# Retention chunks in plain float32 on half arrays, with the decay factored out of the mask

## The chip, the cores and the metric

One core of a Trainium2 chip. The time is the device time of one execution in microseconds; the times before are those of three runs, and one further execution was profiled.

## The reference

Three stages in a row, all in float32. The diff touches the first alone.

```python
# 1. retention; batch 2, 8 heads, 768 steps, head size 64
gamma = 1.0 - 2.0 ** (-5.0 - np.arange(H))
for t in range(S):
    state = gamma[None, :, None, None] * state + einsum('bhd,bhe->bhde', k[:, :, t], v[:, :, t])
    y[:, :, t] = scale * einsum('bhd,bhde->bhe', q[:, :, t], state)
# 2. mixture of experts, one expert of 8 for each of the 1536 tokens, with a capacity of 384
expert_idx = np.argmax(x @ w_gate, axis=1)      # tokens go to their expert's slots in order
y = np.maximum(disp[e] @ w1[e], 0) @ w2[e]      # 512 -> 1024 -> 512, for each expert
out[i] = gate_w[i] * y[expert_idx[i], pos[i]]
# 3. four experts, all of them for every token
out += p[:, e:e + 1] * (np.maximum(x @ w1[e], 0.0) @ w2[e])
```

## The kernel before, in words

The order of the instructions on each engine is that of the program text; each engine takes its instructions in that order, and nothing reorders them but the waits for data and buffers.

Retention works on 12 chunks of 128 steps (6 for each batch; `NCH` = 6, `NT` = 12). For a chunk `i`, all eight heads at once, there are these steps, named by their functions:

- `st_Q`: splits the transposed q and k, each 128 x 512, into a high and a low part of the type fp32r, so that products of nearly float32 precision come from three fast passes. The q parts are put into `qpad`, which is zero wherever a head's other partner has its rows, so that a pair of heads shares one 128-row product. ScalarE writes the high part of q (line 215), VectorE subtracts for the low part (line 216, two instructions of 64 x 512 for each chunk); k's parts are by ScalarE (line 207) and GpSimd (line 208).
- `st_S`: the products of q and k (line 258, twelve instructions, columns 256 wide), into two banks of PSUM, and from there into `sd` with a product with `dec` (VectorE, line 264), which is the causal mask and the decay inside the chunk together, a table of 128 x 1024. GpSimd makes `kg`, which is k times a power of the decay (line 238), and `qg`, which is q times one (line 246).
- `st_U`: k times v summed over the chunks of a batch, in one bank that is held (line 280), copied by ScalarE to the state `st` (line 288). The last chunk of a batch (c = 5) needs none.
- `st_O`: the state product, called I in what follows (line 298, not for the first chunk of a batch), and sd times v (line 308), called O, into one bank, copied to `xT` by ScalarE (line 317).
- `x_pe`: called X; xT is transposed, with the logits beside it, by four products with `iw` (line 339). VectorE reduces the logits (line 345, 353), ScalarE copies the rows to `xk` (line 349), SP writes them to `xd` in memory (line 352).
- `x_dve`, `r_pe`, `r_dve`, `g_pe`: choice of the expert, rank of the token in it, slot lists: many small operations, nearly all on VectorE.

One trip `it` of the loop takes U and O of chunk `it - 1`, S of chunk `it`, the splits of chunk `it + 1`, the loads of chunk `it + 3`, X of chunk `it - 2`, the slots of chunk `it - 4` and the ranks of chunk `it - 3`, in this order. In trips 8 and 9 a block of weights of the second stage is split besides (ScalarE line 106, VectorE line 107). Loads of q and k, and of k and v, go through pools of three buffers each, all on SP's queue. After the loop come O(11), with X(10) and the ranks of 9 between its two halves, then the slots, a gather of the first expert's rows from `xd` (`gidx0`, line 468; `xe0`, line 471), and the first expert's transposed input, whose parts come from the gather (line 498) and from the last two chunks in place (line 489).

The rest of the kernel is the two stages of experts, three fp32r passes each, products of 224 columns for the slots of an expert in the second stage (lines 804 and 828) and of 512 in the third (lines 857 and 878).

Of the kernel before, what the change touches and what calls it, by code (L numbers as in the profile page):

```python
# [37 lines left out]
C_GK = C_D + 1024  # L38
# [12 lines left out]
def tile_retention_moe_moe(ctx: ExitStack, tc, qkv, cst, gqt, a1, a2, b1, b2, dp, out, cap):  # L51
# [89 lines left out]
    with ExitStack() as actx:  # L141
        pa = actx.enter_context(tc.tile_pool(name="pa", bufs=1))
        pq = actx.enter_context(tc.tile_pool(name="pq", bufs=3))
# [4 lines left out]
        gqs = pa.tile([P, NCH - 1, 512], F32, name="gqs")  # L148
# [3 lines left out]
        dec = cdec[:, C_D:C_GK].rearrange("p (j x) -> p j x", j=2)  # L152
# [6 lines left out]

        qpad = [pa.tile([P, 2, 4, 2, P], F32R, name=f"qpad{b}") for b in range(2)]  # L160
# [16 lines left out]
        nc.vector.memset(qpad[0].bitcast(F32), 0.0)  # L177
        nc.gpsimd.memset(qpad[1].bitcast(F32), 0.0)
        load_qk(0)
        load_kv(0)  # L180
        nc.sync.dma_start(out=cdec, in_=cst[:, 0:C_IW])
        load_qk(1)
        load_kv(1)
        load_gq(0)
        load_qk(2)
        nc.sync.dma_start(out=iw.rearrange("p a b -> p (a b)"), in_=cst[:, C_IW:C_U])
        load_kv(2)
        load_gq(1)
# [11 lines left out]
        def st_Q(i):  # L200
            qk = qk_t[i]
            qT = qk[:, 0].rearrange("p (h t) -> p h t", h=4)
            ks = p2.tile([P, 2, 512], F32R, tag="ks", name=f"ks{i}")
            live[i] = {"ks": ks}
            qp = qpad[i % 2]
            def split_k():
                (nc.scalar.copy if i > 1 else nc.vector.tensor_copy)(ks[:, 0], qk[:, 1])
                nc.gpsimd.tensor_tensor(
                    out=ks[:, 1], in0=qk[:, 1], in1=ks[:, 0].bitcast(F32), op=ALU.subtract
                )  # L210

            def split_q():
                for j in range(2):
                    r = slice(64 * j, 64 * j + 64)
                    nc.scalar.copy(qp[r, 0, :, j], qT[r])  # L215
                    nc.vector.tensor_tensor(  # L216
                        out=qp[r, 1, :, j], in0=qT[r], in1=qp[r, 0, :, j].bitcast(F32),
                        op=ALU.subtract,
                    )

            if i == 2:
                split_q()
                split_k()
            else:
                split_k()
                split_q()

        def st_S(i):
            qk = qk_t.pop(i)
            kv = kv_t.pop(i)  # L230
            c = i % NCH
            d = live[i]
            d["v"] = kv[:, 1]
            ks = d.pop("ks").rearrange("p s (h t) -> p s h t", h=4)
            qp = qpad[i % 2].rearrange("p s h j t -> p s h (j t)")
            if c < NCH - 1:
                kg = p2.tile([P, 8, HD], F32, tag="kg", name=f"kg{i}")
                nc.gpsimd.tensor_tensor(
                    out=kg, in0=kv[:, 0].rearrange("p (h d) -> p h d", h=8),
                    in1=gk[:, c].rearrange("p (h d) -> p h d", d=1).to_broadcast([P, 8, HD]),  # L240
                    op=ALU.mult,
                )
                d["kg"] = kg
            if c > 0:
                qg = p2.tile([P, 512], F32, tag="qg", name=f"qg{i}")
                (nc.vector if i < 3 else nc.gpsimd).tensor_tensor(
                    out=qg, in0=qk[:, 0], in1=gqs[:, c - 1], op=ALU.mult
                )
                d["qg"] = qg
            sd = p2.tile([P, 2, 512], F32, tag="sd", name=f"sd{i}")  # L250
            d["sd"] = sd
            bks = [bank(f"S{i}_{g}") for g in range(2)]
            steps = [(n, hp) for hp in range(4) for n in range(3)]
            if i < 3:
                steps.sort()
            for n, hp in steps:
                a, b = PASS[n]
                nc.tensor.matmul(  # L258
                    out=bks[hp // 2][:, (hp % 2) * SL:(hp % 2 + 1) * SL],
                    lhsT=ks[:, a, hp], rhs=qp[:, b, hp], start=(n == 0 and hp % 2 == 0),  # L260
                    stop=True, skip_group_check=True,
                )
            for g in range(2):
                nc.vector.tensor_tensor(out=sd[:, g], in0=bks[g], in1=dec[:, g], op=ALU.mult)
# [3 lines left out]
        def st_U(i):  # L268
            c = i % NCH
            if c == NCH - 1:  # L270
                return
            if c == 0:
                u_ps[0] = bank(f"U{i}", "u")
            u = u_ps[0][:, 0:KD * HD].rearrange("p (a d) -> p a d", a=KD)
            kg = live[i].pop("kg")
            v = live[i]["v"]
# [12 lines left out]

        def st_O(i, between=None):  # L290
            d = live[i]
            c = i % NCH
            bk = bank(f"O{i}")
            sd, v = d.pop("sd"), d.pop("v")
            if c > 0:
                qg = d.pop("qg")
                for hp in range(4):
                    nc.tensor.matmul(
                        out=bk[:, hp * P:(hp + 1) * P], lhsT=st[c % 2][:, hp],
                        rhs=qg[:, hp * P:(hp + 1) * P], start=(hp == 0), stop=False,  # L300
                        skip_group_check=True,
                    )
            if between:
                between()
            for hp in range(4):
                for j in range(2):
                    h = 2 * hp + j
# [22 lines left out]
        def x_pe(i):  # L330
# [21 lines left out]
            nc.sync.dma_start(out=xd[1 + i * P:1 + (i + 1) * P], in_=xk)  # L352
# [70 lines left out]
        for it in range(NT):  # L423
            if it >= 1:
                st_U(it - 1)
                st_O(it - 1)
            if it == 0:
                st_Q(0)
            st_S(it)
            if it + 1 < NT:  # L430
                st_Q(it + 1)
            if it + 3 < NT:
                load_qk(it + 3)
                if it + 2 < NCH - 1:
                    load_gq(it + 2)
                load_kv(it + 3)
# [23 lines left out]
        def between():  # L460
            x_pe(NT - 2)
            r_pe(NT - 3)

        st_O(NT - 1, between)
# [440 lines left out]
def consts(cap):  # L905
# [8 lines left out]
    dm = np.zeros((P, 4, 2, P))  # L914
# [3 lines left out]
    for hd in range(H):  # L918
        hp, j = divmod(hd, 2)
        g = g32[hd]  # L920
        dm[:, hp, j] = np.where(t >= s, scale * g ** np.maximum(t - s, 0), 0.0)
        gk[:, :, hd] = g ** -(ch[None, :] + s + 1.0)
        gq[:, j, :, hp] = scale * g ** (ch[:, None, None] + t[None] + 1.0)
    c[:, C_D:C_GK] = dm.reshape(P, 1024)
# [8 lines left out]
    return c, gq[1:].astype(np.float32).reshape(NCH - 1, P, 512)  # L933
# [61 lines left out]
```

## Time and profile before

| | |
|---|---|
| median of three runs | 802.54 us (801.21 to 802.81) |
| the profiled execution | 802.98 us |
| its span, first to last instruction | 801.2 us |
| mean granted TensorE clock | 0.993 |
| TensorE busy | 779.7 us, 97% of the span |
| VectorE, ScalarE, GpSimd busy | 338.7, 224.7, 93.4 us |

A busy time is the sum of the times from an instruction's start to its end; matmuls overlap in the array and their ends are modelled, so a group's start to the next group's start says what it costs TensorE. A float32 matmul is two records in this trace, an fp32r one is one. PE is TensorE, PEld its weight loads, DVE VectorE, ACT ScalarE, POOL GpSimd; SPq is SP's queue of transfers. The granted clock is a share of 2.4 GHz.

### The profile page before, as it was taken

To read this page: it belongs to the slowest core of one execution; us is meant where nothing else is said; L and a number is where in the kernel's file an instruction comes from. 1 tells how busy PE (TensorE), PEld (TensorE's weight loads), DVE (VectorE), ACT (ScalarE), POOL (GpSimd) and SP (SyncE) were. 2 spreads that over 40 slices of the span, in tenths; PEclk is the share of its full clock that TensorE was granted. 3 is DMA by queue.
4 is the path that set the end of the run, shared out by engine and by line. 5 is a ranking of instruction groups with operands and counts; after the bars stand their busy time and mean duration, and the time that the engine had idled before them with its cause. 6 is when DMAs were issued, how large, how long until landed. Compare 5 with 4: busy or idle time off the path is not lost.

```text
span 801.2 us, 11248 instructions
## 1 busy us (share of the span) xinstructions
PE 779.7 (97%) x4700; PEld 678.9 (85%) x4701; DVE 338.7 (42%) x550; ACT 224.7 (28%) x351; POOL 93.4 (12%) x81
## 2 busy tenths in 40 slices
PE   8987899999999999999999999999999999999996
PEld 5876899999999988888888888888888888888886
DVE  7999786766666531212351221243121235122121
ACT  5555455555545320202230110312020223011010
POOL 6564323212200000000000000000000000000101
PEclk9999999999999999999999999999999999999999
DMA  9784567676666510000150000033000011000001
GB/s 325 268 275 160 171 220 261 208 221 204 209 187 186 183 53 1 1 0 1 53 157 1 1 0 1 5 105 101 1 0 1 1 53 52 27 27 13 40 2 51
DMA packets 24873, 76.64 MB, mean 96 GB/s; under 512 B 4945, under 2 KB 5217, under 8 KB 24818
## 3 DMA queue, kind: packets, MB, share of 16 engines
q1 hardware_dynamic: 20016, 68.21, 26.2%
q0 software_dynamic: 2672, 7.44, 2.9%
q8 instruction: 38, 0.62, 0.3%
q10 hardware_dynamic: 2130, 0.23, 0.2%
q14 instruction: 17, 0.14, 0.1%
HBM read 69.53 MB, written 6.34 MB: 95 GB/s over the span
## 4 chain that ended last, share of the span: by engine, by line
PE 87%; issue 1%; DMA 0%; POOLq 0%; DVE 0%
PE n L857 33%; PE n L878 32%; PE m L804 11%; PE m L828 11%; PE T L678 1%; DMA out_dram<-acc,tl 0%; POOLq L991 0%; DVE acc L889 0%; POOLq L894 0%
## 5 line engine op out<-in xcount | busy, mean ns | idle before, releaser
L857 PE MATMUL n<-x2h,w 128*128 128x512 f32 x768 | 238.4, 389 | 0.0
L857 PEld LDWEIGHTS n<-x2h,w 128*128 128x128 f32 x768 | 144.2, 188 | 30.0
L857 PE MATMUL n<-x2l,w 128*128 128x512 f32 x384 | 149.4, 389 | 0.0
L107 DVE TENSOR_TENSOR w<-raw,w 128x1024 fp32r<-128x1024 f32 x96 | 118.6, 1245 | 18.6 <-ACT w L106 18.5
L106 ACT CAST w<-raw 128x1024 fp32r<-128x1024 f32 x96 | 98.3, 1046 | 0.5 <-DVE tmpc L728 0.4
L889 DVE SCALAR_TENSOR_TENSOR acc<-n,tl,acc 128x512 f32<-128x512 f32 (+1 forms) x37 | 27.3, 737 | 156.7 <-PE n L878 156.7
L804 PE MATMUL m<-xet,w 128*128 128x224 f32 x768 | 88.9, 277 | 2.1 <-issue 1.7
L804 PEld LDWEIGHTS m<-xet,w 128*128 128x128 f32 x768 | 88.1, 195 | 2.4 <-issue 1.8
L857 PEld LDWEIGHTS n<-x2l,w 128*128 128x128 f32 x384 | 72.1, 188 | 14.9
L894 POOL DMA_INDIRECT out_dram<-acc,tl x12 | 11.5, 962 | 571.0 <-DVE acc L889 571.0
L787 ACT ACTIVATE g_0h<-n 128x512 fp32r<-128x512 f32 x12 | 7.2, 598 | 252.7 <-PE n L857 252.7
L258 PE MATMUL S<-qpad,ks 128*128 128x256 f32 x144 | 23.8, 301 | 9.4 <-DVE qpad L216 8.8
L216 DVE TENSOR_TENSOR qpad<-qk,qpad 64x512 fp32r<-64x512 f32 x24 | 31.4, 1307 | 2.3 <-ACT qpad L215 1.9
L258 PEld LDWEIGHTS S<-qpad,ks 128*128 128x128 f32 x144 | 18.8, 191 | 14.5 <-DVE qpad L216 11.3
L884 DVE TENSOR_SCALAR acc<-n,tl 128x512 f32<-128x512 f32 x12 | 9.0, 751 | 51.2 <-PE n L878 51.2
L878 PE MATMUL n<-w,g_1h 128*128 128x512 f32 (+1 forms) x98 | 29.8, 385 | 0.0
L878 PE MATMUL n<-w,g_2h 128*128 128x512 f32 (+1 forms) x98 | 29.8, 385 | 0.0
L878 PE MATMUL n<-w,g_7h 128*128 128x512 f32 (+1 forms) x98 | 29.8, 385 | 0.0
L878 PE MATMUL n<-w,g_3h 128*128 128x512 f32 (+1 forms) x98 | 29.7, 385 | 0.0
L878 PE MATMUL n<-w,g_4h 128*128 128x512 f32 (+1 forms) x98 | 29.7, 385 | 0.0
L878 PE MATMUL n<-w,g_5h 128*128 128x512 f32 (+1 forms) x98 | 29.7, 385 | 0.0
L878 PE MATMUL n<-w,g_6h 128*128 128x512 f32 (+1 forms) x98 | 29.7, 385 | 0.0
(186 smaller groups left out, 1220.7 us busy)
## 6 DMA issues: line engine op xcount, KB each, us to landing
raw<-a SPq DMA_DIRECT2D x64, 512.0 KB, 4.2
raw<-b SPq DMA_DIRECT2D x32, 512.0 KB, 3.6
qk<-qkv SPq DMA_DIRECT2D x12, 512.0 KB, 5.8
kv<-qkv SPq DMA_DIRECT2D x12, 512.0 KB, 5.5
xd<-xk SPq DMA_DIRECT2D x12, 256.0 KB, 3.7
gqs<-gqt SPq DMA_DIRECT2D x5, 256.0 KB, 6.1
cdec<-cst SPq DMA_DIRECT2D x1, 536.0 KB, 5.9
iw<-cst SPq DMA_DIRECT2D x1, 272.0 KB, 7.4
```

Of the source, the lines that this page charges most:

```text
L106: nc.scalar.copy(w[:, 0], r)
L107: nc.vector.tensor_tensor(out=w[:, 1], in0=r, in1=w[:, 0].bitcast(F32), op=ALU.subtract)
L216: nc.vector.tensor_tensor(out=qp[r, 1, :, j], in0=qT[r], in1=qp[r, 0, :, j].bitcast(F32), op=ALU.subtract,)
L258: nc.tensor.matmul(out=bks[hp // 2][:, (hp % 2) * SL:(hp % 2 + 1) * SL], lhsT=ks[:, a, hp], rhs=qp[:, b, hp], start=(n == 0 and hp % 2 == ...
L678: nc.tensor.transpose(bks[g][:, (2 * q + b) * P:(2 * q + b + 1) * P], t[:, b, (2 * g + q) * P:(2 * g + q + 1) * P], ident,)
L804: nc.tensor.matmul(out=bk[:, ff * SL:ff * SL + SM], lhsT=w[:, sw, k, ff * P:(ff + 1) * P], rhs=x[:, sx, k, 0:SM], start=(k == 0 and n == 0 ...
L828: nc.tensor.matmul(out=bk[:, q * SL:q * SL + SM], lhsT=w[:, sw, k], rhs=hs[k // 2][sh][:, hcols], start=(k == 0 and n == 0), stop=(k == KF ...
L857: nc.tensor.matmul(out=bk, lhsT=w[:, sw, k, ff * P:(ff + 1) * P], rhs=x2[sx][:, k, g * 512:(g + 1) * 512], start=(k == 0 and n == 0), stop ...
L878: nc.tensor.matmul(out=bk[:, 0:width], lhsT=hs[k][sh][:, t * P:(t + 1) * P], rhs=w[:, sw, k % 2, cols], start=(k == 0 and n == 0), stop=(k ...
L884: nc.vector.tensor_scalar(out=acc[i][:, cols], in0=bk[:, 0:width], scalar1=sc, scalar2=None, op0=ALU.mult,)
L889: nc.vector.scalar_tensor_tensor(out=acc[i][:, cols], in0=bk[:, 0:width], scalar=sc, in1=acc[i][:, cols], op0=ALU.mult, op1=ALU.add,)
L894: nc.gpsimd.indirect_dma_start(out=out, out_offset=bass.IndirectOffsetOnAxis(ap=tl[:, i, 4:5].bitcast(I32), axis=0), in_=acc[i], in_offset ...
```

## The change

The decay g^(t-s) between two steps of a chunk is written as g^(t+1) times g^-(s+1), with the powers counted from the start of the batch. The second factor goes into v (`vg`, GpSimd, where `kg` was), the first one and the scale are applied to the finished output (`gqs`, now for all six chunks), and of `dec` there is left a causal mask of zeros and ones, 128 x 128, read for all heads. The constants that are loaded with it shrink from 536 KB to 88 KB and go to ScalarE's queue.

With no decay inside, q and k go into the products as they are loaded: `st_Q`, `qpad`, `ks` and `qg` are gone, and the products of q and k are float32 matmuls on 64 rows, the even heads of the pairs on rows 0 to 63 and the odd ones on rows 64 to 127, each into a bank of its own. U takes k and vg, O takes vg and sd, I takes q itself.

The state product has its own function `st_I`, ahead of U in a trip. The output of chunks 0 to 9 is copied by ScalarE from its bank to `ot`, and multiplied by `gqs` to `xT` on GpSimd; of chunks 10 and 11 VectorE multiplies straight from the bank (chunk 11 in two halves). The pools of the loads have five buffers each, and the write of `xk` to `xd` is issued by ScalarE in place of SP.

```diff
-        pq = actx.enter_context(tc.tile_pool(name="pq", bufs=3))
+        pq = actx.enter_context(tc.tile_pool(name="pq", bufs=5))
...
-        dec = cdec[:, C_D:C_GK].rearrange("p (j x) -> p j x", j=2)
+        causal = cdec[:, C_D:C_GK].rearrange("p (o t) -> p o t", o=1).to_broadcast([P, 4, P])
...
         load_qk(0)
+        nc.scalar.dma_start(out=cdec, in_=cst[:, 0:C_IW])
         load_kv(0)
-        nc.sync.dma_start(out=cdec, in_=cst[:, 0:C_IW])
         load_qk(1)
+        load_gq(0)
         load_kv(1)
...
-        def st_Q(i):
...
         def st_S(i):
             qk = qk_t.pop(i)
             kv = kv_t.pop(i)
             c = i % NCH
...
+            vg = p2.tile([P, 8, HD], F32, tag="vg", name=f"vg{i}")
+            nc.gpsimd.tensor_tensor(
+                out=vg, in0=kv[:, 1].rearrange("p (h d) -> p h d", h=8),
+                in1=gk[:, c].rearrange("p (h d) -> p h d", d=1).to_broadcast([P, 8, HD]),
+                op=ALU.mult,
+            )
             sd = p2.tile([P, 2, 512], F32, tag="sd", name=f"sd{i}")
...
+            live[i] = {"sd": sd, "vg": vg, "k": kv[:, 0], "q": qk[:, 0]}
+            bks = [bank(f"S{i}_{j}") for j in range(2)]
+            for hp in range(4):
+                cols = slice(hp * P, (hp + 1) * P)
+                for j in range(2):
+                    r = slice(64 * j, 64 * j + 64)
+                    nc.tensor.matmul(
+                        out=bks[j][:, cols], lhsT=qk[r, 1, cols], rhs=qk[r, 0, cols],
+                        start=True, stop=True,
+                    )
+            for j in range(2):
+                nc.vector.tensor_tensor(
+                    out=sd[:, j].rearrange("p (h t) -> p h t", h=4),
+                    in0=bks[j].rearrange("p (h t) -> p h t", h=4), in1=causal, op=ALU.mult,
+                )
...
-                        out=u[64 * j:64 * j + 64, hp], lhsT=kg[:, h],
-                        rhs=v[:, h * HD:(h + 1) * HD], start=(c == 0 and hp == 0),
+                        out=u[64 * j:64 * j + 64, hp], lhsT=k[:, h * HD:(h + 1) * HD],
+                        rhs=vg[:, h], start=(c == 0 and hp == 0),
...
+        def st_I(i):
             c = i % NCH
-            bk = bank(f"O{i}")
-            sd, v = d.pop("sd"), d.pop("v")
+            bk = live[i]["o"] = bank(f"O{i}")
+            q = live[i].pop("q")
             if c > 0:
...
+        def st_O(i):
...
                     nc.tensor.matmul(
                         out=bk[64 * j:64 * j + 64, hp * P:(hp + 1) * P],
-                        lhsT=v[:, h * HD:(h + 1) * HD],
-                        rhs=sd[:, h // 4, (h % 4) * P:(h % 4 + 1) * P],
+                        lhsT=vg[:, 2 * hp + j], rhs=sd[:, j, hp * P:(hp + 1) * P],
                         start=(c == 0 and hp == 0), stop=True, skip_group_check=True,
                     )
             xT = p2.tile([P, 512], F32, tag="xT", name=f"xT{i}")
-            w = 256 if i == NT - 1 else 512
-            for o in range(0, 512, w):
-                nc.scalar.copy(xT[:, o:o + w], bk[:, o:o + w])
+            if i < NT - 2:
+                ot = p2.tile([P, 512], F32, tag="ot", name=f"ot{i}")
+                nc.scalar.copy(ot, bk)
+                nc.gpsimd.tensor_tensor(out=xT, in0=ot, in1=gqs[:, c], op=ALU.mult)
+            else:
+                w = 256 if i == NT - 1 else 512
+                for o in range(0, 512, w):
+                    nc.vector.tensor_tensor(
+                        out=xT[:, o:o + w], in0=bk[:, o:o + w], in1=gqs[:, c, o:o + w],
+                        op=ALU.mult,
+                    )
...
-            nc.sync.dma_start(out=xd[1 + i * P:1 + (i + 1) * P], in_=xk)
+            nc.scalar.dma_start(out=xd[1 + i * P:1 + (i + 1) * P], in_=xk)
...
             if it >= 1:
+                st_I(it - 1)
                 st_U(it - 1)
                 st_O(it - 1)
-            if it == 0:
-                st_Q(0)
             st_S(it)
-            if it + 1 < NT:
-                st_Q(it + 1)
...
-        st_O(NT - 1, between)
+        st_I(NT - 1)
+        x_pe(NT - 2)
+        r_pe(NT - 3)
+        st_O(NT - 1)
         braid(x_dve(NT - 2), r_dve(NT - 3))
```

## Rows read from the trace of the kernel before

**Rows 1.** Busy time by stretch: microseconds and count of each engine, granted clock, DMA.

```profile
50.00:60.00 10.00, 9.11 (x112) 7.90 (x111) 9.80 (x22) 6.37 (x12) 7.63 (x6) 1.00 0.78 263
...
100.00:110.00 10.00, 10.00 (x92) 10.00 (x91) 7.43 (x12) 5.42 (x8) 2.15 (x2) 1.00 0.85 299
```

**Rows 2.** Timeline of one trip, TensorE: start, length, instruction, count, idle before.

```profile
49.25 1.09 PE L339 MATMUL X<-iw,xT 128*128 128x136 f32 x8
...
50.18 0.19 PE L411 MATMUL slot_ps<-ohk,at 128*128 128x8 f16 x2
...
50.35 0.69 PE L280 MATMUL U<-kv,kg 128*64 128x64 f32 x16
...
50.97 1.16 PE L298 MATMUL O<-qg,st 128*128 128x128 f32 x8
...
52.05 1.09 PE L308 MATMUL O<-sd,kv 128*64 128x128 f32 x16
...
53.08 0.39 PE L258 MATMUL S<-qpad,ks 128*128 128x256 f32 x1
...
53.98 1.58 PE L258 MATMUL S<-qpad,ks 128*128 128x256 f32 x11 [0.52 <-DVE qpad L216]
```

**Rows 3.** Timeline, two windows: U of chunk 1 and U of chunk 10.

```profile
14.24 0.69 PE L280 MATMUL U<-kv,kg 128*64 128x64 f32 x16
...
72.17 0.69 PE L280 MATMUL U<-kv,kg 128*64 128x64 f32 x16
```

**Rows 4.** Timeline of the trip of rows 2, the other engines and SP's queue.

```profile
50.65 1.27 POOL L208 TENSOR_TENSOR ks<-qk,ks 128x512 fp32r<-128x512 f32 x1 [1.72 <-ACT ks L207]
...
51.29 2.64 DVE L216 TENSOR_TENSOR qpad<-qk,qpad 64x512 fp32r<-64x512 f32 x2
51.88 1.50 POOL L238 TENSOR_TENSOR kg<-kv,cdec 128x512 f32<-128x512 f32 x1
...
53.34 1.74 POOL L246 TENSOR_TENSOR qg<-qk,gqs 128x512 f32<-128x512 f32 x1
...
54.84 0.33 SPq L352 DMA_DIRECT2D xd<-xk  x1
...
55.49 0.59 ACT L317 COPY xT<-O 128x512 f32<-128x512 f32 x1
```

**Rows 5.** Groups by line and shape, VectorE: busy us, mean ns, idle before.

```profile
L216 DVE TENSOR_TENSOR qpad<-qk,qpad 64x512 fp32r<-64x512 f32 x24 | 31.4, 1307 | 2.3 <-ACT qpad L215 1.9
...
L264 DVE TENSOR_TENSOR sd<-S,cdec 128x512 f32<-128x512 f32 x24 | 15.4, 682 | 1.1 <-PE S L258 1.1
```

**Rows 6.** Waits of SP's queue: what for, us in total, times, longest.

```profile
SPq L170 <- PE O L308: 20.7, 7, 3.6
```

**Rows 7.** Timeline of the start.

```profile
1.25 4.60 PE L80 MATMUL warm<-fill 128*128 128x512 f16 x11 [1.25 <-DVE fill L175]
...
7.77 1.16 POOL L238 TENSOR_TENSOR kg<-kv,cdec 128x512 f32<-128x512 f32 x1 [1.01 <-DMA cdec<-cst]
...
10.38 1.92 PE L308 MATMUL O<-sd,kv 128*64 128x128 f32 x16
```

**Rows 8.** TensorE's busy time by stretch at the start, with the granted clock.

```profile
6.00:8.00 2.00, 0.74 (x4) 1.00 1.02 361
...
10.00:11.00 1.00, 1.00 (x18) 0.50 1.04 377
```

**Rows 9.** Timeline of a trip with a weight split.

```profile
60.10 2.20 DVE L107 TENSOR_TENSOR w<-raw,w 128x1024 fp32r<-128x1024 f32 x1
...
62.42 0.65 ACT L349 COPY xk<-X 128x256 f32<-128x256 f32 x2 [3.47 <-DVE lgs L345]
```

**Rows 10.** Timeline of the end, two windows: O(11), the slot list, the gathered rows.

```profile
81.13 1.09 PE L308 MATMUL O<-sd,kv 128*64 128x128 f32 x16
...
82.71 0.15 DVE L468 CAST gidx<-slot_ps 128x2 int32<-128x2 f32 x1
...
89.62 1.16 PE L498 MATMUL T0x<-ident,xe 128*128 128x128 f32 x8 [0.22 <-DMA xe<-xd,gidx]
```

More of the change, by code (lines that the diff above doesn't have):

```diff
@@ L37 @@
 C_D = 0
-C_GK = C_D + 1024
+C_GK = C_D + P
 C_IW = C_GK + NCH * 8
@@ L147, in tile_retention_moe_moe @@
         cdec = pa.tile([P, C_IW], F32, name="cdec")
-        gqs = pa.tile([P, NCH - 1, 512], F32, name="gqs")
+        gqs = pa.tile([P, NCH, 512], F32, name="gqs")
         iw = pa.tile([P, KD, 136], F32, name="iw")
@@ L158, in tile_retention_moe_moe @@
         )
-        qpad = [pa.tile([P, 2, 4, 2, P], F32R, name=f"qpad{b}") for b in range(2)]
         qk_t, kv_t = {}, {}
@@ L176, in tile_retention_moe_moe @@
         nc.scalar.copy(zero[:, 0:1], fill[0:1, 0:1])
-        nc.vector.memset(qpad[0].bitcast(F32), 0.0)
-        nc.gpsimd.memset(qpad[1].bitcast(F32), 0.0)
         load_qk(0)
+        nc.scalar.dma_start(out=cdec, in_=cst[:, 0:C_IW])
         load_kv(0)
-        nc.sync.dma_start(out=cdec, in_=cst[:, 0:C_IW])
         load_qk(1)
+        load_gq(0)
         load_kv(1)
-        load_gq(0)
+        nc.sync.dma_start(out=iw.rearrange("p a b -> p (a b)"), in_=cst[:, C_IW:C_U])
         load_qk(2)
-        nc.sync.dma_start(out=iw.rearrange("p a b -> p (a b)"), in_=cst[:, C_IW:C_U])
+        load_gq(1)
         load_kv(2)
-        load_gq(1)
         nc.scalar.dma_start(out=tie, in_=cst[:, C_TIE:C_TOK])
@@ L198, in tile_retention_moe_moe @@
         live = {}
-        def st_Q(i):
[L201 to L226, printed above, removed]
         def st_S(i):
@@ L231, in st_S @@
             c = i % NCH
[L232 to L241, printed above, removed]
-                )
-                d["kg"] = kg
@@ L244, in st_S @@
[L244 to L264, printed above, removed]
+            vg = p2.tile([P, 8, HD], F32, tag="vg", name=f"vg{i}")
@@ new lines, in st_S @@
+            nc.gpsimd.tensor_tensor(
[3 more added lines that the diff above has]
+            )
+            sd = p2.tile([P, 2, 512], F32, tag="sd", name=f"sd{i}")
+            live[i] = {"sd": sd, "vg": vg, "k": kv[:, 0], "q": qk[:, 0]}
[8 more added lines that the diff above has]
+                    )
@@ L274, in st_U @@
             u = u_ps[0][:, 0:KD * HD].rearrange("p (a d) -> p a d", a=KD)
-            kg = live[i].pop("kg")
-            v = live[i]["v"]
+            k = live[i].pop("k")
+            vg = live[i]["vg"]
             for hp in range(4):
@@ L299, in st_O @@
                         out=bk[:, hp * P:(hp + 1) * P], lhsT=st[c % 2][:, hp],
-                        rhs=qg[:, hp * P:(hp + 1) * P], start=(hp == 0), stop=False,
+                        rhs=q[:, hp * P:(hp + 1) * P], start=(hp == 0), stop=False,
                         skip_group_check=True,
                     )
-            if between:
-                between()
+        def st_O(i):
+            d = live[i]
+            c = i % NCH
+            bk = d.pop("o")
+            sd, vg = d.pop("sd"), d.pop("vg")
             for hp in range(4):
                 for j in range(2):
-                    h = 2 * hp + j
                     nc.tensor.matmul(
                         out=bk[64 * j:64 * j + 64, hp * P:(hp + 1) * P],
-                        lhsT=v[:, h * HD:(h + 1) * HD],
-                        rhs=sd[:, h // 4, (h % 4) * P:(h % 4 + 1) * P],
+                        lhsT=vg[:, 2 * hp + j], rhs=sd[:, j, hp * P:(hp + 1) * P],
                         start=(c == 0 and hp == 0), stop=True, skip_group_check=True,
@@ L424, in tile_retention_moe_moe @@
             if it >= 1:
+                st_I(it - 1)
                 st_U(it - 1)
                 st_O(it - 1)
-            if it == 0:
-                st_Q(0)
             st_S(it)
-            if it + 1 < NT:
-                st_Q(it + 1)
             if it + 3 < NT:
                 load_qk(it + 3)
-                if it + 2 < NCH - 1:
+                if it + 2 < NCH:
                     load_gq(it + 2)
@@ L458, in tile_retention_moe_moe @@
             braid(*seqs)
-        def between():
-            x_pe(NT - 2)
-            r_pe(NT - 3)
-        st_O(NT - 1, between)
+        st_I(NT - 1)
+        x_pe(NT - 2)
+        r_pe(NT - 3)
+        st_O(NT - 1)
         braid(x_dve(NT - 2), r_dve(NT - 3))
@@ L913, in consts @@
     c = np.zeros((P, C_RNK + SL), np.float32)
-    dm = np.zeros((P, 4, 2, P))
     gk = np.zeros((P, NCH, H))
@@ L920, in consts @@
         g = g32[hd]
-        dm[:, hp, j] = np.where(t >= s, scale * g ** np.maximum(t - s, 0), 0.0)
         gk[:, :, hd] = g ** -(ch[None, :] + s + 1.0)
         gq[:, j, :, hp] = scale * g ** (ch[:, None, None] + t[None] + 1.0)
-    c[:, C_D:C_GK] = dm.reshape(P, 1024)
+    c[:, C_D:C_GK] = (t >= s)
     c[:, C_GK:C_IW] = gk.reshape(P, NCH * H)
@@ L932, in consts @@
     c[:, C_RNK:] = np.where(np.arange(SL) < min(cap, SM), np.arange(SL), -1)[None, :]
-    return c, gq[1:].astype(np.float32).reshape(NCH - 1, P, 512)
+    return c, gq.astype(np.float32).reshape(NCH, P, 512)
 def pack(inputs):
```

3 lines of the change are left out of this document (removed).

## The prediction

> **What bounds the kernel now.** Three views were read, in this order: busy time by stretches, the timeline of one trip of the retention loop, and the timeline of the loop's start and end. The stretches [rows 1] show two different kernels. From 100 us on TensorE is busy in the whole of every stretch, so nothing the diff touches can shorten that part; what the first 90 us lose or win moves the end by as much. Between 50 and 60 us it is VectorE that has 9.80 of 10 us, TensorE 9.11, and the latter counts the pipeline's tail of each matmul.
>
> One trip of the loop on TensorE [rows 2] reads, from start to start: X with slots and ranks 1.10 us (49.25 to 50.35), U 0.62, the state product I 1.08, O 1.03 (52.05 to 53.08), then S: one record, 0.52 us of idle put down to VectorE's qpad, and eleven more in 1.58 with their tail. With some 1.5 for S TensorE needs 5.3 us for a trip, and from U(1) at 14.24 to U(10) at 72.17 [rows 3] a trip takes (72.17 - 14.24)/9 = 6.44. The rest is VectorE: its two qpad subtractions take 2.64 us in this trip [rows 4] and 31.4 us over the twelve trips [rows 5]; S cannot finish before them, and the next trip's S product, slot and rank work queue behind them.
>
> **The change part by part.** *VectorE.* The 24 subtractions go, 31.4/12 = 2.6 us of a trip; the sd products stay, two at 0.68 us [rows 5], with the mask in place of the decay. 6.44 - 2.6 = 3.8 us a trip is left at most, so VectorE stops being the bound. *ScalarE* loses its q and k casts, keeps st, xk and the copy out of O's bank (0.59 us [rows 4], now called ot), and takes the issue of the xd write: 0.33 us on SP's queue [rows 4], now behind xk and ahead of the next st. *GpSimd* loses ks and qg, trades kg for vg (same shape and broadcast), and gets the product xT = ot x gq. *SP* no longer waits for xk, and with five buffers the kv loads no longer wait for O, which cost their queue 20.7 us in all [rows 6]; so loads run ahead of the compute. No price on the path for those after the first two trips.
>
> *S on TensorE.* Twelve records of 256 columns become sixteen of 128 columns (each float32 matmul shows two), on 64 contraction rows each, upper and lower half in turn. No row shows half arrays of that kind. The nearest are O, sixteen records on two column halves in 1.03 us [rows 2], and X, eight on the full array from 49.25 to 50.18, 0.116 us each, so sixteen in 1.86. If the halves run beside each other S takes O's 1.03, if not 1.86. I take 1.03, since O shows that two halves of this array do run side by side in float32, 0.064 us a record. A trip of TensorE is then 1.10 + 1.08 + 0.62 + 1.03 + 1.03 = 4.86 us, else 4.86 + 0.83 = 5.69.
>
> The Trainium skill speaks against that choice: "TensorE: Matmul & The Clock Gate", section "LDWEIGHTS (loading the stationary operand)", says that a load costs by its columns whatever the number of its rows; sixteen loads of 128 columns would then cost as on the full array, and only the page's remark that loads of other row groups overlap stands for 1.03. By that rule the trip is the 5.69, by O's row 4.86; no run here shows it yet.
>
> *The new ring.* What was VectorE's is not all given to TensorE, because GpSimd now stands inside the chain: O(i) needs vg(i), ot copies O(i), xT(i) waits for ot, and vg(i+1) is queued behind xT(i) on GpSimd, with U(i+1) and O(i+1) waiting for it. Once round: U to O 0.62, O to its end 1.09 [rows 2], to ScalarE and to GpSimd 0.1 each (an estimate, twice the 0.05 that VectorE's 51.29 + 2.64 = 53.93 stands ahead of TensorE's 53.98 [rows 2, 4]), ot 0.59, xT, vg, to TensorE 0.05. For xT the rows are 1.27 (ks, two plain operands, beside sd) and 1.74 (qg, beginning beside qpad's subtraction) [rows 4]; for vg 1.16 (kg beside the end of one subtraction and then nothing [rows 7]) and 1.50 (kg wholly beside it [rows 4]). xT will lie beside sd, as ks does, and vg beside small operations, nearer to the 1.16. So I take 1.27 and 1.25: 0.62 + 1.09 + 0.1 + 0.59 + 0.1 + 1.27 + 1.25 + 0.05 = 5.07, with ends 4.98 and 5.79. That is just longer than TensorE's 4.86, so the period is 5.1 us: 1.3 less than 6.44, half of what the subtractions free. TensorE will idle some 0.2 us a trip ahead of U.
>
> *The start.* S(0) no longer waits for splits: it follows the warm matmuls at 1.25 + 4.60 = 5.85 [rows 7] and ends at 6.9. vg(0) needs kv0 and the constants; the latter landed third, at 7.77 [rows 7], and are now a sixth the size, so I put both at 6.5 (between 5.85 and 7.77). vg(0) to 7.8, U(0) to 8.5, O(0) 1.1 us, or 1.92 as in the trace, where the granted clock was at its lower level, 0.50 or 1.2 GHz, in that stretch [rows 7, 8]: to 9.6 or 10.4; ot 0.7, xT 1.4, vg(1) 1.25 with their gaps: U(1) at 13.0 to 13.8. I take 13.5; 14.5 if loads of the second trip come late. The old U(1) was at 14.24, so the start gives little.
>
> *The two trips with a weight split.* L107 took 2.20 us [rows 9]. It still stands between sd and X's reductions on VectorE; xk on ScalarE waits for these reductions (3.47 us of idle in [rows 9]), and behind xk now stand the xd issue, st and ot, which is in the ring. From O's end: S ends at 1.1, sd at 2.4, the split at 4.6, reductions and xk 5.5, issue 5.9, st 0.76 to 6.7, ot from 6.7 where the ring wants it at 5.2: 1.5 us in each of the two trips, 3.0 in all, and nothing if the split slips by faster. Chunk 5 has no U: 0.6 less.
>
> *The sum.* U(10) at 13.5 + 9 x 5.1 + 3.0 - 0.6 = 61.8. From there to O(11) runs TensorE alone: U, O, S, X with ranks, I, X with ranks: 0.62 + 1.03 + 1.03 + 1.10 + 1.08 + 1.10 = 5.96, so O(11) starts at 67.8, where it was 81.13 [rows 10]: 13.3 us.
>
> *The end gives some back.* xT(11) goes from ScalarE to VectorE, which holds it in program order ahead of the slot and rank operations of trips 10 and 9. These ran while O(11) ran, and gidx was copied at 82.71, 1.6 us after O(11) began [rows 10]. Now they wait for O's end (1.2 us) and two halves of some 0.4 us (half of sd's 0.68, and a fixed part), then take the 1.1 us that they took: gidx at 3.1. The gather that follows had TensorE wait at 89.62 already [rows 10], so nothing covers the delay: 1.5 us back. Net 13.3 - 1.5 = 11.8 us. The profiled execution took 802.98 (span 801.2), so 791.2; it lies 0.4 over the median, and the forecast on that scale is 791.
>
> **The rivals.** (a) S's halves don't overlap: trips of 5.69, 0.6 x 9 more, and 0.83 in the last stretch: 797. For it speaks that all full-array float32 records stand at their own pace; against it O's halves. (b) GpSimd keeps the slower durations, 1.74 and 1.50: trips of 5.79, 0.7 x 9 more: 797 as well. The slow rows lay beside the subtractions, which the diff removes [rows 4]. (c) The splits and the end cost nothing: 4.5 less, 786 to 787. (d) Slower: the granted clock falls to its lower level in the retention. The half arrays work in S, U and O now, and the clock did fall once in the loop: it was 0.50 from 10 to 11 us, after a stretch from 6 to 8 us in which TensorE was busy for 0.74 of 2 us [rows 8]. There O(0) took 1.92 for 1.09 [rows 2, 7], so a trip becomes 4.86 x 1.92/1.09 = 8.6 us and the kernel 791 + 9.5 x 3.5 = 824. It decides once a trip is over 5.1 + 11.8/9 = 6.4 us. Against it: in the middle of the loop the clock stood at 1.00, 2.4 GHz (50 to 60 us in [rows 1]) through 0.5 us and more of idle in a trip; now it idles less.
>
> **How the numbers follow.** Forecast 0.60, its own range 788 to 794 (start 0.5 either way, splits 0 to 3, vg 1.16 to 1.4); (a) 0.20; (b) 0.08; (c) 0.07; (d) 0.05. A change of 0.2% is about what a measurement of this kernel can tell from none. From 786 to 798 lie all but (d) and the edges of (b), where the late loads and a 5.79 us trip add up. (a) to (c) are all faster; of what is left, some 0.02 lands within 0.2%.
>
> **What would show it.** Right: no records at the old lines 207, 208 and 216; U to U near 5.1 us in the trips without split; TensorE's idle ahead of U put down to GpSimd's vg; S to X near 1.03 us; xT and vg near 1.27 and 1.25; O(11) near 68 us; gidx 3 us after it; granted clock 1.00 from 20 to 65 us. Wrong: S records 0.11 us apart (a), GpSimd products at 1.5 us and more (b), 0.50 in the clock's column in the middle of the loop (d), or an idle VectorE ahead of ub that waits for ScalarE's loads behind the deep SP queue, which none of the terms above has.

## The result, and the profile after

The changed kernel takes 790.05 us (median of four runs, 789.56 to 792.03), the kernel before 801.93 on the same chips: a ratio of 0.9856, with 0.9840 to 0.9873 as its 95% interval. The profiled execution went from 802.98 to 790.38 us, its span from 801.2 to 788.6, so 12.6 us are there to be found. In every row below, "idle before" in brackets ends the line, with what ended it.

The same stretches as in [rows 1], by engine:

```profile
50.00:60.00 10.00, 8.04 (x114) 7.37 (x114) 7.77 (x25) 4.62 (x11) 6.53 (x5) 1.00 0.57 210
100.00:110.00 10.00, 10.00 (x92) 10.00 (x91) 8.52 (x15) 4.88 (x8) 2.93 (x2) 1.00 0.55 181
```

VectorE is down from 9.80 to 7.77 of 10 us; after 100 us TensorE is busy throughout, as before. One trip of TensorE against [rows 2], from its timeline, with U of chunks 1, 2, 9 and 10 [rows 3] around it:

```profile
12.30 0.69 PE L237 MATMUL U<-vg,kv 128*64 128x64 f32 x16 [0.85 <-POOL vg L201]
...
18.73 0.69 PE L237 MATMUL U<-vg,kv 128*64 128x64 f32 x16 [1.75 <-POOL vg L201]
...
42.67 0.69 PE L237 MATMUL U<-vg,kv 128*64 128x64 f32 x16
43.19 1.05 PE L266 MATMUL O<-sd,vg 128*64 128x128 f32 x16
44.16 1.16 PE L213 MATMUL S<-qk 64*128 64x128 f32 x16
45.25 1.19 PE L304 MATMUL X<-iw,xT 128*128 128x136 f32 x8
...
46.39 1.14 PE L253 MATMUL O<-qk,st 128*128 128x128 f32 x8
47.45 0.69 PE L237 MATMUL U<-vg,kv 128*64 128x64 f32 x16
...
54.27 0.69 PE L237 MATMUL U<-vg,kv 128*64 128x64 f32 x16 [1.96 <-POOL vg L201]
...
59.05 0.69 PE L237 MATMUL U<-vg,kv 128*64 128x64 f32 x16
```

A trip without a disturbance takes 4.78 us (42.67 to 47.45) and has no idle time on TensorE: U 0.52, O 0.97, S 1.09, X with slots and ranks 1.14, I 1.06. The two rows with 1.75 and 1.96 us of idle end trips 2 and 9 (a trip is counted here from one U to the next), which took 6.43 and 6.82.

The end, against [rows 10], over all engines, and from a view of the branch's own line TensorE's branch into the experts (duration in ns three times, then its start):

```profile
64.79 1.09 PE L266 MATMUL O<-sd,vg 128*64 128x128 f32 x16
...
66.01 0.76 DVE L279 TENSOR_TENSOR xT<-O,gqs 128x256 f32<-128x256 f32 x2 [0.75 <-PE O L266]
...
67.43 0.20 PE L376 MATMUL slot_ps<-ohk,at 128*128 128x8 f16 x2 [1.40 <-DVE at L369]
67.76 0.15 DVE L429 CAST gidx<-slot_ps 128x2 int32<-128x2 f32 x1
...
L530 PEldq COMPARE_BRANCH  x1: 3821/3821/3821, 75.7 to 75.7; - x1
...
75.10 1.16 PE L459 MATMUL T0x<-ident,xe 128*128 128x128 f32 x8 [0.71 <-DMA xe<-xd,gidx]
...
80.00 12.58 PE L765 MATMUL m<-xet,w 128*128 128x224 f32 x96 [3.74 <-ACT w L106]
```

The same place in the kernel before, which [rows 10] did not show:

```profile
L569 PEldq COMPARE_BRANCH  x1: 352/352/352, 90.2 to 90.2; - x1
...
91.22 0.79 PE L804 MATMUL m<-xet,w 128*128 128x224 f32 x5 [0.45 <-PEq L569]
93.69 11.95 PE L804 MATMUL m<-xet,w 128*128 128x224 f32 x91 [1.68 <-issue]
105.48 1.03 PE L678 MATMUL T<-ident,xe 128*128 128x128 f32 x8
```

So the account is: U(10) is 13.1 us earlier than before (59.05 against 72.17), O(11) 16.3 (64.79 against 81.13), T0x 14.5 (75.10 against 89.62), and the end of the first expert's first products ("the first expert" from here on) 13.1: it stands at 105.48 in the kernel before and at 92.41 after. The last store is still issued 13.1 us earlier (782.84 against 795.97); the span shows 12.6, so the missing half microsecond lies behind that issue, and its cause stays open.

### The profile page after: what moved, and what is told of

It reads as the page before. It is cut to its first block, busy times and chain, and to the rows that moved or that the text cites. A ratio compares the mean times of both kernels' runs of the same rounds, so it can differ in the third digit from the quotient of the medians.

```text
span 788.6 us, 11217 instructions
## 1 busy us (share of the span) xinstructions
PE 767.8 (97%) x4748; PEld 669.8 (85%) x4749; DVE 305.4 (39%) x524; ACT 204.5 (26%) x314; POOL 73.7 (9%) x72
## 4 chain that ended last, share of the span: by engine, by line
PE 88%; ACT 0%; DMA 0%; issue 0%; POOLq 0%; DVE 0%
PE n L818 33%; PE n L839 32%; PE m L765 11%; PE m L789 11%; PE T L639 1%; ACT w L106 0%; DMA out_dram<-acc,tl 0%; POOLq L950 0%; DVE acc L850 0%; POOLq L855 0%
## 5 line engine op out<-in xcount | busy, mean ns | idle before, releaser
L107 DVE TENSOR_TENSOR w<-raw,w 128x1024 fp32r<-128x1024 f32 x96 | 117.4, 1233 | 19.2 <-ACT w L106 19.2
L839 PE MATMUL n<-w,g_0h 128*128 128x512 f32 (+1 forms) x98 | 29.7, 385 | 0.0
L789 PE MATMUL m<-h_0h,w 128*128 128x224 f32 x128 | 27.2, 278 | 0.0
L789 PE MATMUL m<-h_2h,w 128*128 128x224 f32 x128 | 26.6, 274 | 0.0
```

The costliest lines, as they stand in the source:

```text
L107: nc.vector.tensor_tensor(out=w[:, 1], in0=r, in1=w[:, 0].bitcast(F32), op=ALU.subtract)
L789: nc.tensor.matmul(out=bk[:, q * SL:q * SL + SM], lhsT=w[:, sw, k], rhs=hs[k // 2][sh][:, hcols], start=(k == 0 and n == 0), stop=(k == KF ...
L839: nc.tensor.matmul(out=bk[:, 0:width], lhsT=hs[k][sh][:, t * P:(t + 1) * P], rhs=w[:, sw, k % 2, cols], start=(k == 0 and n == 0), stop=(k ...
```

## The experiments

Kernels whose name begins with "before" are edits of the kernel before; all others are edits of the changed one. Ratios are to the kernel before on the same chip; the changed kernel's is 0.9856.

**1. Only the subtractions taken out of the kernel before.** The low part of q stays zero, so the products are less exact; all else of the old kernel stays.

```diff
-                    nc.vector.tensor_tensor(
-                        out=qp[r, 1, :, j], in0=qT[r], in1=qp[r, 0, :, j].bitcast(F32),
-                        op=ALU.subtract,
-                    )
```

> The kernel before without VectorE's 24 subtractions: the low part of q stays zero, all matmuls stay. Theory (these subtractions set the trip): trips go from 6.44 us to TensorE's own 5.3 to 5.4, and the kernel to 791 to 793, most of the gain of the whole change. Rival (the trips are set by TensorE or by GpSimd's products all the same): 800 to 802.

789.62 us, ratio 0.9844 (0.9825 to 0.9863). The timeline of TensorE:

```profile
46.94 1.70 PE L254 MATMUL S<-qpad,ks 128*128 128x256 f32 x12
48.48 1.09 PE L335 MATMUL X<-iw,xT 128*128 128x136 f32 x8
...
49.58 0.69 PE L276 MATMUL U<-kv,kg 128*64 128x64 f32 x16
...
54.93 0.69 PE L276 MATMUL U<-kv,kg 128*64 128x64 f32 x16
```

Trips of 5.35 us (49.58 to 54.93) with TensorE as the bound: S without its wait takes 1.54. VectorE's 24 instructions alone are worth as much as the whole change. All the rest of the change, the faster S among it, comes to nothing net, although its trips are 0.57 shorter: what it wins is lost at other places, which experiments 3 to 10 look for. Against this kernel the changed one is ahead by 3.2 us at O(11) (64.79 for 68.01), by 1.45 at T0x (75.10 for 76.55) and by 0.26 at the first expert's end (92.41 for 92.67).

**2. S's halves one after the other**, not in turn.

```diff
-            for hp in range(4):
-                cols = slice(hp * P, (hp + 1) * P)
-                for j in range(2):
-                    r = slice(64 * j, 64 * j + 64)
+            for j in range(2):
+                r = slice(64 * j, 64 * j + 64)
+                for hp in range(4):
+                    cols = slice(hp * P, (hp + 1) * P)
```

> The changed kernel with the two loops of S exchanged: first the four products on rows 0 to 63, then the four on rows 64 to 127, so that neighbours in TensorE's order share their half. Theory (the halves run side by side only because they alternate): S from 1.09 us to X's start goes to about 1.9; a trip of TensorE from 4.78 to 5.6; the waits ahead of U for vg (6.9 us in all) hide some 4.6 of the twelve times 0.8, so the kernel takes 794 to 796. Rival (each product is as fast alone, or the order does not matter): S stays at 1.09 and the time at 790.

792.13 us, ratio 0.9882 (0.9865 to 0.9898). TensorE's timeline:

```profile
45.68 1.71 PE L213 MATMUL S<-qk 64*128 64x128 f32 x16
47.32 1.19 PE L304 MATMUL X<-iw,xT 128*128 128x136 f32 x8
```

S to X is 1.64 us instead of 1.09, U to U 5.34 instead of 4.78 (44.19 to 49.53). So the products of the two halves overlap more when they alternate than when each half's four come in a row. In the changed kernel the bank of PSUM alternates together with the half, and no run separates the two. The cost is 0.55 and not the expected 0.8, and part of it fills waits for vg that were there anyway: ahead of U these fell from 6.9 to 3.6 us in all.

**3. xT of every chunk on VectorE**, straight from the bank; no ot on ScalarE, and vg alone on GpSimd.

```diff
-            if i < NT - 2:
-                ot = p2.tile([P, 512], F32, tag="ot", name=f"ot{i}")
-                nc.scalar.copy(ot, bk)
-                nc.gpsimd.tensor_tensor(out=xT, in0=ot, in1=gqs[:, c], op=ALU.mult)
-            else:
-                w = 256 if i == NT - 1 else 512
-                for o in range(0, 512, w):
...
+            w = 256 if i == NT - 1 else 512
+            for o in range(0, 512, w):
```

> The changed kernel with xT of all chunks by VectorE straight from O's bank, as chunks 10 and 11 have it; ot and GpSimd's products are gone. Theory (the waits ahead of U come from the ring through ot, xT and vg): U waits for vg in chunk 0 alone, trips keep TensorE's 4.78 us, and the waits of chunks 1, 2, 3, 6 and 9, together 5.96 us, go: 784 to 786. Rival 1 (VectorE, with 0.68 us more in a trip, becomes late and TensorE waits for sd or X's reductions): 789 to 793. Rival 2 (something else holds U, such as the late loads): 789 to 790.

785.66 us, ratio 0.9798 (0.9780 to 0.9817). The groups of U by line, first of the changed kernel, then of this one (busy us, mean ns, idle before):

```profile
L237 PE MATMUL U<-vg,kv 128*64 128x64 f32 x160 | 6.9, 228 | 6.9 <-POOL vg L201 6.9
```

```profile
L237 PE MATMUL U<-vg,kv 128*64 128x64 f32 x160 | 6.9, 228 | 1.6 <-POOL vg L201 1.5
...
54.29 0.69 PE L237 MATMUL U<-vg,kv 128*64 128x64 f32 x16
```

With GpSimd out of the chain the waits for vg fall from 6.9 to 1.5 us, the trip with the split takes 4.78 (49.51 to 54.29) and O(11) starts at 60.04, 4.8 us earlier. A steady trip is no shorter, so there TensorE sets the pace in the changed kernel too; the detour over ot and GpSimd costs only in the disturbed trips.

**4. The write of xk to xd on SP again.** One line: `nc.sync.dma_start` in place of `nc.scalar.dma_start`.

> The changed kernel with the write of xk to xd issued by SP again. Theory (on ScalarE an issue stands ahead of st and ot and waits for another transfer's landing as well as for xk): the wait of chunk 3's U (0.60) goes, in chunk 9 ot comes 0.4 earlier, and the kernel takes 789 to 789.7. Rival 1 (SP, waiting for xk, holds up the loads in spite of the five buffers): 790.5 or more. Rival 2 (no effect): 790.

789.02 us, ratio 0.9822 (0.9809 to 0.9836). Trip 9 takes 6.33 us in place of 6.82 (U at 46.32 and 52.65), and O(11) starts at 63.18 instead of 64.79; part of that is lost behind the branch. ScalarE's issues are thus worth 1.6 us at O(11) while ScalarE is in the chain, and between 1.0 (times) and 2.7 us (ratios) in the total.

**5. The two small loads late.** dps and the zero row, which ScalarE issues at the end of the program's trip 1, ahead of st and ot of trip 2, go to SP in trip 6.

```diff
-                nc.scalar.dma_start(out=dps, in_=dp.rearrange("(i p) e -> p i e", p=P))
-                nc.scalar.dma_start(out=xd[0:1], in_=zero)
+            if it == 6:
+                nc.sync.dma_start(out=dps, in_=dp.rearrange("(i p) e -> p i e", p=P))
+                nc.sync.dma_start(out=xd[0:1], in_=zero)
```

> The changed kernel with two small transfers of trip 1 (the table of the second router and the zero row) issued by SP in trip 6. Theory (ScalarE's issue of them waits for other transfers to land, and st and ot of chunk 1 stand behind it): st(1) follows U(1) at once, about 13 us in place of 14.88, ot(1) at 13.9 in place of 15.65, U(2) comes 1.6 us earlier (17.1), and the kernel takes 788 to 788.8. Rival (chunk 2's loads are late anyway): U(2) stays near 18.5, 790.

790.96 us, ratio 0.9844 (0.9830 to 0.9858): no gain in the total. The place that it was made for did gain: U(2) starts at 17.35 (18.73 in the changed kernel), and the trip takes 4.60. But the stall came back where the loads went. ScalarE's and SP's rows of trip 7, with TensorE's next U behind them:

```profile
35.64 0.65 ACT L314 COPY xk<-X 128x256 f32<-128x256 f32 x2 [1.84 <-DVE lgs L310]
35.79 0.32 SPq L404 DMA_DIRECT2D xd<-zero  x1
...
38.96 0.33 ACTq L317 DMA_DIRECT2D xd<-xk  x1
39.33 0.75 ACT L245 COPY st<-U 64x256 f32<-64x256 f32 x2 [3.04 <-PE S L213]
...
43.14 0.69 PE L237 MATMUL U<-vg,kv 128*64 128x64 f32 x16 [1.24 <-POOL vg L201]
```

xk is done at 36.29, its write is issued at 38.96: ScalarE stands for 2.67 us at the issue, st and ot behind it come late, and that trip takes 6.93 (36.21 to 43.14). The issue comes right after the zero row's write to the same xd; that it waited for this or an older transfer fits, but is not shown. The changed kernel itself has such a stop in trip 3, ahead of its first write of xk (done at 17.31, issued at 19.96), and experiment 3 ahead of its second (22.25 and 24.79), with another write between it and the zero row's: which transfer is waited for stays open.

**6. The last xT behind the rank work.** VectorE's operations of the slots of 10 and the ranks of 9 are put ahead of xT(11).

```diff
-        st_O(NT - 1)
-        braid(x_dve(NT - 2), r_dve(NT - 3))
+        st_O(NT - 1, lambda: braid(x_dve(NT - 2), r_dve(NT - 3)))
```

> The changed kernel with the slot and rank operations of trips 10 and 9 ahead of chunk 11's xT on VectorE, as they ran before the change. Theory (xT(11) holds them up, and the gather of the first expert's rows behind them): gidx comes 1.6 us after O(11)'s start in place of 3.0, TensorE's wait of 1.40 us for the slot list goes, and the T0x products of the gathered rows start 8.7 to 9.0 us after O(11) in place of 10.3: 788.5 to 789. Rival (the gather takes its time from something else, the late writes of xd by ScalarE for one): T0x stays at 10 us or more after O(11), and the kernel at 790.

791.03 us, ratio 0.9850 (0.9829 to 0.9872). The wait of 1.40 us ahead of slot_ps is gone and T0x stands 9.02 us after O(11) (66.89 and 75.91), not 10.31; gidx at 2.25 us misses the 1.6, since its copy is still behind xT(11) on VectorE. Yet nothing is won: in this profile O(11) itself is 2.1 us later, with a granted clock of 0.83 from 50 to 60 us, and the first expert took 13.60 us where it took 12.58 before. That the reorder is worth its 1.3 us is thus seen in its stretch alone, not in a time.

**7. 36 tiny matmuls ahead of U(0).** They cost 0.8 us there (U(0) starts at 8.53 for 7.71); they move all later instructions of TensorE 72 places down its program (a matmul has a weight load).

```diff
                 st_I(it - 1)
+                if it == 1:
+                    bk = bank("tiny", "x0")
+                    for _ in range(36):
+                        nc.tensor.matmul(
+                            out=bk[:, 0:8], lhsT=fill[:, 0:P], rhs=fill[:, 0:8], start=True,
+                            stop=True,
+                        )
                 st_U(it - 1)
```

> The changed kernel with 36 tiny matmuls (8 columns, into an unused bank) ahead of U(0), where TensorE waits for 0.97 us anyway: 72 instructions more in TensorE's stream ahead of the branch after retention. Theory (the 3.8 us of that branch and the five-records-and-stop of the kernel before are fetches of TensorE's program, and their place depends on where the stream stands): the branch takes under 1 us, the first expert starts within 1 us of the last xet part, and the kernel takes 786 to 788.5. Rival (the branch waits for data or for other engines): the branch stays at 3.5 us or more, and the time at 790 to 790.5.

789.05 us (785.38 to 790.01), ratio 0.9831 (0.9802 to 0.9859): in this total the interval takes in no change against 0.9856. The end, from the branch's line and TensorE's timeline:

```profile
L537 PEldq COMPARE_BRANCH  x1: 925/925/925, 79.3 to 79.3; - x1
...
80.72 10.95 PE L772 MATMUL m<-xet,w 128*128 128x224 f32 x96 [0.84 <-DVE xet L670]
```

The branch takes 0.93 us for 3.82, the first expert starts 2.00 us after T0x (78.72) instead of 4.90, and at 2.4 GHz it takes 10.95. But O(11) is 4.1 us late in the profiled execution (68.92): 0.8 are the tiny matmuls' own, I(3) waits 1.74 us for ot behind a write of xk that ScalarE issues late, and the granted clock is 0.83 from 20 to 30 us. So the times alone do not settle what the place of the branch is worth, and experiment 8 turns it round.

**8. The kernel before, with its branch moved to the place that it has in the changed kernel**: 44 such matmuls, so that 1683 records of TensorE stand ahead of the branch, as in the changed kernel; without them it is 1595.

> The kernel before, with 44 matmuls of 8 columns ahead of U(0), so that TensorE's branch ahead of the experts stands as many instructions from the start of its program as in the changed kernel (1683 instead of 1595); the rest is untouched. Theory (the branch costs by its place in the program, and part of what the end gave back in the changed kernel is this place): the branch takes 3 us and more instead of 0.35, the first expert starts 1.5 to 3 us later than 93.69, and the kernel is 1 to 2 us slower than before, 803 to 805. Rival (the branch is long in the changed kernel because TensorE comes to it earlier, or for what other engines do): branch at 0.35 to 0.9 us and the kernel within 0.7 us of before.

804.99 us, ratio 1.0035 (1.0023 to 1.0046), slower by 0.35%, and clear of noise. Branch and timeline:

```profile
L576 PEldq COMPARE_BRANCH  x1: 3721/3721/3721, 91.9 to 91.9; - x1
...
91.27 1.16 PE L505 MATMUL T0x<-ident,xe 128*128 128x128 f32 x8 [0.35 <-DMA xe<-xd,gidx]
...
96.06 12.58 PE L811 MATMUL m<-xet,w 128*128 128x224 f32 x96 [3.64 <-PEq L576]
108.48 1.04 PE L685 MATMUL T<-ident,xe 128*128 128x128 f32 x8
```

The long branch goes with the place: 3.72 us here in the old kernel. From T0x to the first expert's end it is 17.21 us (91.27 to 108.48), where the old kernel has 15.86 (89.62 to 105.48) and the changed one 17.31. T0x itself is 1.65 us late; most of that is there at U(0) already (11.00 for 9.47), behind the tiny matmuls, which the expectation had left out. Note the 15.86: the old kernel had a stop too, 1.68 us after five records, so the place costs the change 1.4 us and not the 3.5 by which the branches differ. In the other profiles the stretch from T0x to the first expert's end takes 17.2 to 18.4 us with the long branch (experiments 2 to 6 and 10), 16.1 in experiment 1 and 12.8 in experiment 7.

**9. Experiments 3, 5, 6 and 7 together, and then 4 as well.**

> xT of all chunks by VectorE, the slot operations ahead of chunk 11's xT, the two small transfers late on SP, and the 36 tiny matmuls ahead of U(0), all together. Theory (four separate waits, one behind the other, so the savings add up): 785.7 less 1.3 for the end, 0.5 for the small transfers, 2.5 for the branch: 781 to 782. Rival (they share the same slack, such as the gather's landing): 784 to 785.

> The changed kernel with xT on VectorE for all chunks, the last xT behind the rank work, the two small loads late and on SP, 36 tiny matmuls early, and the write of xk to xd on SP as well, so that ScalarE issues no transfer in the loop. Theory (with xT on VectorE the ring has slack, so ScalarE's issues cost nothing any more): within 1 us of the 782.29 of the version without the last edit, trips of 4.78. Rival (the issue still counts, as it did by 1.0 us with xT on GpSimd): 781 or less, O(11) a microsecond ahead of 59.23.

782.29 us, ratio 0.9742 (0.9725 to 0.9759), and 781.87, ratio 0.9739 (0.9723 to 0.9755). The first one's rows of the end:

```profile
L534 PEldq COMPARE_BRANCH  x1: 460/460/460, 70.1 to 70.1; - x1
...
59.23 1.09 PE L266 MATMUL O<-sd,vg 128*64 128x128 f32 x16
...
71.06 10.95 PE L769 MATMUL m<-xet,w 128*128 128x224 f32 x96 [0.45 <-PEq L534]
```

Together the four edits are worth 7.8 us by the times and 9.1 by the ratios, of which experiment 3 alone had 4.4 and 4.7: the profile has O(11) at 59.23 after trips of 4.78, and the first expert starts 11.8 us later in place of 15.2. The write on SP adds nothing any more, as the theory had it: with xT on VectorE ScalarE's copies are out of the chain.

**10. Three buffers in the pools of the loads** in place of five (`bufs=3` for `pq`).

> The changed kernel with three buffers in the pools of the loads, as before the change, instead of five. Theory (the loads are off the path after the first two trips, whichever the depth): 789 to 791, trips still 4.78 us, U waits for vg alone; SP's queue waits for O again, some 20 us in all. Rival (the deep queue is part of the gain, since loads that start only when O has freed a buffer land late for S): a wait for the q and k load ahead of S in each trip, trips of 5.2 us and more, 793 to 796. Second rival (the deep queue costs something, since an issue on ScalarE stands still for older transfers that the deep queue has put ahead of it): trip 2 of 5.2 us instead of 6.43 and 788.

790.10 us, ratio 0.9841 (0.9821 to 0.9861). SP's queue waits for O again, less than in [rows 6], and no wait of TensorE comes of it:

```profile
SPq L164 <- PE O L253: 11.9, 5, 3.4
```

Trips stay at 4.78; trip 2 takes 6.19 (U at 12.47 and 18.66), so most of its stall has nothing to do with the depth of the queue. Both rivals fall: no effect of the depth on the total is seen here either way.

## Why the prediction held, and where its terms were off

**What bound the old kernel is what was predicted; what bounds the new one is not.** The 24 subtractions were the bound, and their removal alone gives the whole 12 us (experiment 1). With them gone, the prediction had the ring through ScalarE and GpSimd (5.07 us) as just longer than TensorE's own work (4.86), with some 0.2 us of idle time ahead of U in each trip. In the trace TensorE sets the steady trip, 4.78, and that idle time is not there.

**S.** 1.09 us against a predicted 1.03, so rival (a) is out. The rule of the Trainium skill that spoke against it ("TensorE: Matmul & The Clock Gate", section "LDWEIGHTS (loading the stationary operand)": a load costs by its columns, not its rows) comes nearest to the trace where halves do not alternate: 1.64 us for S in experiment 2, where sixteen records at X's pace would be 1.86. The same page's remark that a load can go ahead of running matmuls when the row groups do not conflict fits the kernel as written; experiment 2 does not show whether the half or the bank decides.

**The ring.** Predicted 5.07 with GpSimd in it, so a period of 5.1 and idle time ahead of U. Measured: vg(i) takes 1.04 and xT 1.28 in a steady trip:

```profile
44.34 0.58 ACT L274 COPY ot<-O 128x512 f32<-128x512 f32 x1 [0.19 <-PE O L266]
...
45.00 1.28 POOL L275 TENSOR_TENSOR xT<-ot,gqs 128x512 f32<-128x512 f32 x1 [2.51 <-ACT ot L274]
...
46.23 1.04 POOL L201 TENSOR_TENSOR vg<-kv,cdec 128x512 f32<-128x512 f32 x1
```

From U at 42.67 the next vg is done at 47.27, that is 4.60 later, just inside TensorE's own 4.78. The step that was off is "I take 1.27 and 1.25", with the sum of 5.07 that follows from it: xT was right, vg 0.2 too long, and U with O is 0.14 shorter than in [rows 2]. Rival (b) is out by the same rows.

**Trip 2** was not in the sum. ScalarE's queue has two small transfers ahead of st and ot. The second takes 1.41 us to issue, and st and ot begin only behind it:

```profile
13.43 1.41 ACTq L403 DMA_DIRECT2D xd<-zero  x1
14.88 0.74 ACT L245 COPY st<-U 64x256 f32<-64x256 f32 x2 [4.97 <-PE O L266]
15.65 0.58 ACT L274 COPY ot<-O 128x512 f32<-128x512 f32 x1
```

The trip is 1.65 us too long (6.43 less 4.78), and takes 4.60 when experiment 5 moves them. The transfers were there in the old kernel; what is new is that ScalarE now stands in a chain without slack.

**The splits.** Predicted 1.5 us in each of two trips. In the first, the predicted path ran: xk waited 2.61 us for the reductions behind L107, and ot(8) came at 50.29, where the pace of the steady trip (44.34 less 42.67 after U at 47.45) wants 49.12: 1.17 late. The second added its share in another place:

```profile
46.56 1.80 DVE L107 TENSOR_TENSOR w<-raw,w 128x1024 fp32r<-128x1024 f32 x1
...
48.48 0.65 ACT L314 COPY xk<-X 128x256 f32<-128x256 f32 x2 [2.61 <-DVE lgs L310]
...
50.29 0.58 ACT L274 COPY ot<-O 128x512 f32<-128x512 f32 x1
...
51.85 1.46 DVE L107 TENSOR_TENSOR w<-raw,w 128x1024 fp32r<-128x1024 f32 x1 [0.42 <-ACT w L106]
52.19 2.03 POOL L201 TENSOR_TENSOR vg<-kv,cdec 128x512 f32<-128x512 f32 x1
```

vg took 2.03 beside the split for 1.04 without. Both fell into trip 9, which has 2.04 too much; the second split's own ScalarE delay cost nothing, U being late already. So 2.0 in place of 3.0.

**The sum to O(11).** The start gave 1.2 us more than I had (U(1) at 12.30 for 13.5: O(0) ran at 2.4 GHz in 1.05 us, not 1.92, and the gaps were shorter). From U(1) to U(10) I had 45.9 + 3.0 - 0.6 = 48.3; it took 46.75, which is nine trips of 4.78, with 1.65 more in trip 2, 0.62 in trip 3 (U waits 0.60 for vg, behind a late issue on ScalarE) and 2.04 in trip 9, and 0.58 less in trips 5 and 6 together, where U(5) and I(6) are missing. The last stretch took 5.74 for 5.96. So O(11) came 3.0 us earlier than the 67.8 that I had.

**The end gave back more.** gidx stands 2.97 us after O(11), predicted 3.1, by the predicted path: slot_ps waits 1.40 for VectorE behind xT. T0x is 1.8 later against O(11) than before, for 1.5. What the sum lacked is the stretch behind it, from T0x to the first expert's end: 17.31 us for 15.86, another 1.45, which experiment 8 puts down to the place of TensorE's branch.

Together: 3.0 us better to O(11), and 2.2 worse behind it (0.3 at T0x, 1.45 at the branch, 0.5 behind the last store's issue): 12.6 in place of 11.8. The total was right partly by luck, because these two cancel. Rival (c) had named the right sign for the loop, but not for the end. (d) did not come in this profile, where the granted clock stood at 1.00 through the loop; in experiment 6 it came for one stretch (0.83 from 50 to 60 us), and trip 10 took 6.35 us there for 4.78.

## What to carry to other kernels

When a bound is taken away, list what each engine does in the odd trips (issues, splits, first and last) and not only in the steady one: here the steady trip came out 0.3 us better than forecast and three odd places (trip 2, trip 9 and the branch) cost 5 us, which four small edits won back with more. Keep an engine that also issues transfers out of the chain that sets the pace, or give that chain slack. Before an unrolled program's edit is credited or blamed for a microsecond at a branch, look at how long the branch itself took, since the same edit moves it to another place in the program.

## What the runs showed of the hardware

**TensorE's branch costs by its place.** It took 0.35 us with 1595 records ahead of it (kernel before, experiment 1), 3.3 to 3.9 with 1683 to 1689 (the changed kernel and experiments 2 to 6, 8, 10), 0.93 with 1755 and 0.46 with 1762 (7, 9). The Trainium skill ("Runtime: NRT & Kernel Launch", section "Instruction fetch mechanics") states that a taken branch to a target outside the pieces of program already fetched waits for a transfer; the trace agrees in that the wait is there or not by the place alone (experiments 7 and 8), and gives the price that no row of before had. The transfer itself is not seen in any run.

**What such a stop does to the clock.** In the changed kernel TensorE stood still for 3.74 us ahead of the first expert, and the granted clock was below 1.00 behind it, part of the stretch at 1.2 GHz:

```profile
80.00:90.00 10.00, 10.00 (x75) 10.00 (x76) 5.62 (x6) 3.03 (x5) 2.55 (x2) 0.83 0.92 325
```

The first expert took 12.58 us there, and 12.58 to 13.69 in the other kernels with a stop of 3.2 us and more; where the stop was 0.84 or 0.45 (experiment 7 and the first of 9) it took 10.95. Yet the second kernel of 9, with a stop of 0.45, also took 12.58, with 0.83 from 70 to 80 us: the length of this stop does not decide it alone.

**VectorE and GpSimd beside each other.** vg began 0.34 us after L107 and ended 0.91 after its end (53.31 to 54.22), near the 1.04 that it takes by itself. Experiment 3 has the same: L107 at 49.01 takes 1.21, and vg, begun at 49.05, takes 2.07. The other way round, L107 took 1.80 at 46.56, where vg had begun first, and ended 1.09 after vg (47.27 to 48.36), near its own 1.21. The Trainium skill ("SBUF — State Buffer", section "SBUF: two separate sides") has a GpSimd operation and a VectorE operation with two SBUF inputs share a port pair that whichever starts first holds for the whole instruction. These rows agree to within some 0.1 us; xT of 1.28 beside sd, which reads a bank of PSUM, shows no such wait.
